# Seven products instead of eight for the third column group of the first layer, its weight sums streamed through one room

## The chip, the cores and the metric

The kernel runs on one core of a Trainium2 chip. The metric is the device time of one execution in microseconds. Before the change it is 1401.8 us, the median of three runs (1399.14 to 1404.3). The engines are named as in the profile: PE is TensorE, PEld its weight loads, DVE VectorE, ACT ScalarE, POOL GpSimd, SP the queue that issues nearly all DMAs.

## The reference

An attention with a threshold, then a bilinear feed-forward layer, all in float32:

```python
scores = scale * np.matmul(q, k.transpose(0, 1, 3, 2))          # (8, 8, 576, 576), head_dim 64
thresh = np.max(scores, axis=-1, keepdims=True) - tau
scores = np.where(scores >= thresh, scores, -1000000000.0)
attn = np.exp(scores - np.max(scores, axis=-1, keepdims=True))
attn = attn / (np.sum(attn, axis=-1, keepdims=True) + 1e-09)
attn_out = np.matmul(attn, v)
x = attn_out.transpose(0, 2, 1, 3).reshape(4608, 512)
out = ((x @ w_a) * (x @ w_b)) @ w_out                           # w_a, w_b: 512 x 1536; w_out: 1536 x 512
```

## The kernel before

**Units and slots.** Attention is cut into units of 128 query rows of a pair of heads. There are 32 pairs (batch, two heads) and 144 units; each passes through a pipeline of slots: `scores` (matmuls at L404, then row maxima L411 and thresholds L412 on DVE), `weigh` (exponential L432 on ACT, mask and sum L435 on DVE), `reciprocal` (L446, L448) and `normalise` (L454), `turn_blocks` (transposes L502 on DVE, then stores to the DRAM scratch `swap`), `turn_back` (loads into `wT`) and `weighted` (matmuls with v, "pv", L546; copies into x at L553 and L554). All matmuls are 64 x 64 pieces, four of them at a time in the four quadrants of the array; a 512-long contraction is 8 chunks of 64.

**Feed-forward blocks.** When 256 rows of x are complete (a half of a batch, or the tails of four batches), they become a block; there are 18. `exchange_blocks` makes the copy with swapped partition halves (`xs`) and, once the weight sums exist, sums of x (`x_sums`, L576) on POOL. A block is a generator, `ffn`, that yields after every few matmuls. `advance(cols)` runs it for so many columns of PE time, and the slot loop calls it in four portions per slot, so feed-forward matmuls lie between the attention's. The order on each engine is the order in which the program emits instructions (`keep_order`), so a waiting instruction holds all behind it on its engine. `held` keeps some of the columns back for the time behind pv.

**First layer.** The 1536 columns are three groups of 512 (`NG`). For a group, x times (w_a, w_b) is taken as a 2 x 2 block product: token halves and halves of the contraction on one side, halves of the contraction and the two weights on the other. Eight products would be needed; `sevens_of` does it in seven (numbered 1, 2, 6, 7, 4, 5, 3), with sums of weights (`first_sums`, L707) and sums of x. Two groups (`SEVENS`) are done so together: products 1, 6, 7, 4 are added up in one tile of on-chip accumulation memory, 2 on its own, 5 and 3 in another. ACT and DVE read the results out (L799, L803, L806, L811, L815, L820, L824), and the gated halves h are finished by DVE (product 4) and by POOL (two multiplications, L826, recorded at the helper's L712). The third group is done by `plain`: four steps, each the whole contraction for 128 columns of one weight and 256 tokens (L854, read out at L860 and L862). Three of the four steps are put between the products of the other two groups (`yield from plain(0)` to `plain(2)`), the fourth behind product 3. The sums of the two groups stay in SBUF, in `first_sb` and `more_sb`.

**The last blocks.** When attention is over (`state["over"]`), three tiles named `tw` are free; POOL computes the third group's sums into them, and `everything` does all three groups by seven products. The last two blocks go that way, 14 the way above, and the first two are plain throughout.

**Second layer.** It is also done in seven products (L920), in the pairs (1, 4), (2, 5), (7, 6) and (3), each over six pieces f, with weight sums t1, t2 and t4 in `sums_sb`. Product 1 reads the first 128 tokens of half the columns, product 4 the second 128 tokens of the other half, with t4; product 6 is the only reader of t2. Sums of h between them are on POOL (L883). The results go through tiles `kept` (tag `osb`, four rooms of 128 x 512, which the first layer's `u3` tiles use too) to DRAM.

**DMA.** `post` puts a transfer on a list and `pump` issues them on SP, each bound to the PE instruction that was last emitted; `flush` issues those at once that the next operation reads.

Of the kernel before, what the change touches and what calls it, by code (L numbers as in the profile page):

```python
# [10 lines left out]
FP32 = mybir.dt.float32  # L11
# [3 lines left out]
ALU = mybir.AluOpType  # L15
# [39 lines left out]
def kernel(  # L55
# [180 lines left out]
    for F in range(NF):  # L236
# [4 lines left out]
             "layer": False, "paced": False, "all": False, "turn": 0, "due": NPIECES, "wide": True, "slot": 0, "reading": False, "first": 0}  # L241
# [5 lines left out]
    sums_of = sums_sb.rearrange("p (f n w) -> p f n w", n=3, w=CH)  # L247
    QUARTER = HP * CH
    first_u32 = const.tile([P, 3 * QUARTER], U32, name="first_u32")
# [430 lines left out]
    def weight_sums(n, z):  # L680
        f = slice(z * NG, (z + 1) * NG)
        w = wo_sb.rearrange("p (f k) (c w) -> p f k c w", k=2, c=2)[:, f]
        w11, w12, w21, w22 = (w[:, :, k, c] for k in range(2) for c in range(2))
        t1, t2, t4 = (sums_of[:, f, m] for m in range(3))
        out, a, b = ((t1, w12, w11), (t2, w22, t1), (t4, w21, t2), (w12, w22, w12))[n]
        nc.gpsimd.tensor_tensor(out, a, b, op=ALU.subtract)


    def sums_at(group, m):
        if group == SEVENS:  # L690
            return last_sums[m]
        return (first_sb, more_sb)[group][:, m * QUARTER:(m + 1) * QUARTER]

    def last_rooms():
        for _ in range(3):
            t = work.tile([P, 2 * NB, Q], FP32, tag="tw", bufs=TW_BUFS, name="s")
            last_sums.append(t.rearrange("p n e -> p (n e)")[:, 0:QUARTER])

# [10 lines left out]
    def sevens_of(x, hg, plain):  # L709
# [13 lines left out]
        def s(m):  # L723
            return [[sums_at(NG - 1 - g, m)[:, k * CH:(k + 1) * CH] for k in range(HP)] if g >= of_all or everything
                    else None for g in range(NG)]
# [41 lines left out]
        if everything:  # L767
# [28 lines left out]
            return  # L796
        a = banks(nf * P, "pab")
# [10 lines left out]
        yield from plain(0)  # L808
# [4 lines left out]
        yield from plain(1)  # L813
# [8 lines left out]
        yield from plain(2)  # L822
# [4 lines left out]
        yield done  # L827

    def ffn(xT, what):
# [39 lines left out]
        if len(xT) == 4:  # L869
            rest = [(f, 0, HALF, (w,)) for f in range((NG - SEVENS) * n) for w in both]  # L870
            if state["all"]:
                yield from sevens_of(xT, h_of, None)
            else:
                yield from sevens_of(xT, h_of, lambda k: plain(rest[k:k + 1]))
                yield from plain(rest[3:])
        else:
            yield from plain([(*step, both) for step in steps])
# [3 lines left out]
        if state["sums"]:  # L881
# [4 lines left out]
            t1, t2, t4 = (sums_of[:, :, m] for m in range(3))  # L886
# [17 lines left out]
            for both in ((4, 1) if state["all"] else (1, 4), (2, 5), (7, 6), (3,)):  # L904
# [3 lines left out]
                for m, part in ((m, part) for m in both for part in range(1 + last)):  # L908
# [5 lines left out]
                    for f in range(NF // 2):  # L914
                        ht = hs[f // 2 * 2 + k][:, f % 2]
                        for r in range(2):
                            rows = slice(r * D, (r + 1) * D)
                            for c in range(2):
                                t0 = u * P + c * D
                                nc.tensor.matmul(po[c * D:(c + 1) * D, r, y, cut], ht[rows, t0:t0 + D],  # L920
                                                 other[rows, f, cut], start=(f == 0), stop=(f == NF // 2 - 1))
                        left -= CH // (1 + last)
                        if m == both[-1] and 4 in both and f == NF // 2 - 1:
                            h_sums((1, 1), (0, 1), (1, 1), ALU.add)
                            h_sums((0, 1), (0, 0), (0, 1), ALU.subtract)
                            h_sums((0, 0), (1, 1), (0, 0), ALU.subtract)
                        if m == 2 and f == NF // 2 - 1:
                            h_sums((1, 0), (1, 0), (0, 0), ALU.subtract)
                            state["layer"] = False
                            exchange_blocks()  # L930
                        if last and f == NF // 2 - 1:
                            for r in range(2):
                                nc.vector.tensor_tensor(final[:, cut], final[:, cut], po[:, r, 0, cut],
                                                        op=ALU.add)
                                if not part:
                                    second(r)
# [81 lines left out]
    def cost():  # L1018

        return BLOCK_COLS - (NF // 2 * CH if state["sums"] else 0) - (SEVENS * 2 * HP * P if state["first"] >= 3 * SEVENS else 0)  # L1020
# [3 lines left out]
    def advance(cols):  # L1024
        running["owed"] += cols
        while running["owed"] > 0:
            if running["ffn"] is None:
# [8 lines left out]
                if state["over"] and not state["all"]:  # L1036
                    first_sums(3, SEVENS)
                    state["all"] = True
# [73 lines left out]
    n = 0  # L1112
# [4 lines left out]
    for g in range(len(units) + PV_LAG):  # L1117
# [54 lines left out]
        if g > BY_PE:  # L1172
# [3 lines left out]
            if now:  # L1176
                held = 384 - (PORTIONS[2] + PORTIONS[3]) * pace + NSLOT * sum(width(*x) for x in now) // 2
                held = min(max(held, 0.0), 384)
# [58 lines left out]
        if g > first[HP] + 1 and not converting and state["first"] < 3 * SEVENS:  # L1237
            first_sums(state["first"] % 3, state["first"] // 3)
            state["first"] += 1
    state["over"] = True  # L1240
    last_rooms()
    for n in range(3):
        first_sums(n, SEVENS)
# [38 lines left out]
```

## Time and profile before

| what | value |
|---|---|
| median of the runs | 1401.8 us (1399.14 to 1404.3) |
| the profiled execution's own time | 1400.57 us |
| its span, first to last instruction | 1398.8 us |
| mean granted clock of TensorE | 0.998 |
| PE busy | 1361.5 us, 97% of the span |
| DVE, ACT, POOL busy | 1013.9, 680.8, 492.8 us |
| DMA moved | 223.21 MB |
| attention and feed-forward together | about 250 to 1264 us |
| feed-forward alone | about 1264 us to the end |

A busy share is the time in which an engine had an instruction under way. Line numbers (L750) are those of the kernel before. A group's line has its count, the busy time, the mean of one, and the idle time before it with what ended that. The chain is the work that ended last, followed back from the last instruction. A row of DMA issues has its count, the size of one and the median time from issue to landing.

### The profile page before, as it was taken

The numbers are of one execution on the slowest core, as the hardware profiler recorded it, in microseconds if no ns is written. First come the engines' busy times: TensorE is split into PE (matmuls) and PEld (weight loads), VectorE is DVE, ScalarE is ACT, GpSimd is POOL, SyncE is SP. The second block draws the span as 40 slices with busy tenths as digits, with TensorE's granted clock in tenths as the row PEclk, the third lists the DMA queues.
The fourth block names the chain that finished last, engine by engine and source line by source line (L and its number), as shares of the span: only waits on it lengthen the run. The fifth ranks groups of instructions, "written<-read, shape, count | busy, mean of one in ns | idle before, by whom it ended". The sixth has DMA issues, their size and how long they took to land.

```text
span 1398.8 us, 76307 instructions
## 1 busy us (share of the span) xinstructions
PE 1361.5 (97%) x33836; PEld 1258.5 (90%) x33836; DVE 1013.9 (72%) x2205; ACT 680.8 (49%) x1248; POOL 492.8 (35%) x675
## 2 busy tenths in 40 slices
PE   7889999999999999999999999999999999999998
PEld 5677588999998799999999999998899998799998
DVE  6999877787777768786767776778777776745425
ACT  6977555545554555544454545454545455431110
POOL 2764543424150607060515142332515060708100
PEclk9999999999999999999999999999999999999999
DMA  9977876667666775676556775566656775550000
GB/s 211 241 212 223 204 206 173 174 170 187 174 154 168 190 192 155 176 190 160 143 143 160 186 180 159 136 190 169 181 130 161 199 190 154 137 146 19 4 19 18
DMA packets 327449, 223.21 MB, mean 160 GB/s; under 512 B 171600, under 2 KB 311632, under 8 KB 327120
## 3 DMA queue, kind: packets, MB, share of 16 engines
q1 hardware_dynamic: 323936, 216.95, 60.1%
q8 instruction: 266, 4.36, 1.3%
q10 hardware_dynamic: 3184, 1.38, 0.4%
q14 instruction: 63, 0.52, 0.1%
HBM read 128.58 MB, written 89.65 MB: 156 GB/s over the span
## 4 chain that ended last, share of the span: by engine, by line
PE 88%; DMA 5%; DVE 4%; SPq 2%; issue 1%; ACT 1%; ACTq 0%; DVEq 0%
PE pab L750 29%; PE po L920 22%; PE pab L854 18%; PE sc L404 9%; PE pv L546 9%; SPq L144 1%; DMA vm<-in_v_dram 1%; DMA wT<-swap 1%; DVE tw L435 1%; DVE mx L411 1%; DMA more_u<-in_moe_w_a_dram 1%; DVE low L311 0%; DMA more_u<-in_moe_w_b_dram 0%; DVE tw L502 0%; DMA sums_u<-in_k_dram 0%
## 5 line engine op out<-in xcount | busy, mean ns | idle before, releaser
L454 ACT ACTIVATE tw<-tw,rcp 128x576 f32<-128x576 f32 x272 | 196.1, 768 | 201.3 <-DVE rcp L448 201.3
L411 DVE TENSOR_REDUCE mx<-sc 128x1 f32<-128x576 f32 x288 | 204.6, 752 | 121.2 <-PE sc L404 120.9
L432 ACT ACTIVATE tw<-sc,bias,scalars 128x576 f32<-128x576 f32 x288 | 239.6, 832 | 10.4 <-DMA qT<-in_q_dram 0.4
L712 POOL TENSOR_TENSOR h<-h,u 128x512 f32<-128x512 f32 x28 | 35.2, 1277 | 590.4 <-DVE h L824 414.1
L435 DVE SCALAR_TENSOR_TENSOR tw<-sc,thr,tw 128x576 f32<-128x576 f32 x288 | 220.9, 797 | 12.3 <-ACT tw L432 11.9
L920 PE MATMUL po<-wo_sb,h 64*64 64x256 f32 (+1 forms) x3408 | 210.5, 367 | 0.0
L502 DVE STREAM_TRANSPOSE tw<-tw 128x576 f32<-128x576 f32 x272 | 194.4, 752 | 0.8 <-ACT tw L454 0.8
L920 PEld LDWEIGHTS po<-wo_sb,h 64*64 64x64 f32 x3408 | 169.8, 133 | 14.9
L404 PE MATMUL sc<-kT,qT 64*64 64x288 f32 x2016 | 170.3, 404 | 1.8 <-issue 0.9
L546 PE MATMUL pv<-wT,vm 64*64 64x128 f32 (+2 forms) x4896 | 164.0, 275 | 3.7 <-DMA vm<-in_v_dram 1.4
L546 PEld LDWEIGHTS pv<-wT,vm 64*64 64x64 f32 x4896 | 153.2, 133 | 12.0 <-issue 4.0
L920 PE MATMUL po<-sums_u,h 64*64 64x256 f32 x2448 | 156.6, 376 | 0.0
L883 POOL TENSOR_TENSOR h<-h 128x256 f32<-128x256 f32 x168 | 117.2, 731 | 110.9 <-PE po L920 106.1
L750 PE MATMUL pab<-xU,wb_sb 64*64 64x128 f32 x4352 | 137.8, 269 | 0.0
L920 PEld LDWEIGHTS po<-sums_u,h 64*64 64x64 f32 x2448 | 126.1, 133 | 12.3 <-DVE h L862 0.5
L750 PEld LDWEIGHTS pab<-xU,wb_sb 64*64 64x64 f32 x4352 | 133.3, 133 | 1.8 <-ACT h L806 0.5
L404 PEld LDWEIGHTS sc<-kT,qT 64*64 64x64 f32 x2016 | 108.8, 133 | 17.3 <-issue 4.9
L431 ACT ACTIVATE bias<-mx,scalars 128x1 f32<-128x1 f32 x288 | 82.7, 287 | 66.1 <-DVE mx L411 65.6
L553 ACT COPY xT<-pv 128x128 f32<-128x128 f32 (+1 forms) x68 | 17.6, 259 | 193.5 <-PE pv L546 193.5
L750 PE MATMUL pab<-xS,wa_sb 64*64 64x128 f32 x2176 | 108.5, 269 | 0.8 <-issue 0.8
L554 DVE COPY xT<-pv 64x128 f32<-64x128 f32 (+1 forms) x136 | 38.1, 280 | 80.5 <-PE pv L546 79.0
L535 ACT COPY kept<-po 128x512 f32<-128x512 f32 x65 | 34.8, 535 | 120.3 <-PE po L920 106.4
(163 smaller groups left out, 2468.7 us busy)
## 6 DMA issues: line engine op xcount, KB each, us to landing
wT<-swap SPq DMA_DIRECT2D x242, 288.0 KB, 3.8
swap<-tw SPq DMA_DIRECT2D x480, 144.0 KB, 3.1
vm<-in_v_dram SPq DMA_DIRECT2D x128, 72.0 KB, 2.6
swap<-tw SPq DMA_DIRECT2D x128, 72.0 KB, 2.9
kT<-in_k_dram SPq DMA_DIRECT2D x112, 72.0 KB, 3.2
wT<-swap SPq DMA_DIRECT2D x56, 144.0 KB, 3.6
out_dram<-kept SPq DMA_DIRECT2D x27, 256.0 KB, 3.7
qT<-in_q_dram SPq DMA_DIRECT2D x112, 40.0 KB, 2.8
```

The costliest lines, as they stand in the source:

```text
L404: nc.tensor.matmul(sc[m][o * D:o * D + wide, c], qT[r, q0:q0 + wide], kT[r, c * SH:(c + 1) * SH], start=True, stop=True)
L411: nc.vector.tensor_reduce(mx[:, c], sc[j], axis=AX.XY, op=ALU.max)
L431: nc.scalar.activation(bias[:, j:j + 1], mx[:, j:j + 1], AF.Copy, scale=e_nscale)
L432: nc.scalar.activation(wb[j], sb[j], AF.Exp, bias=bias[:, j:j + 1], scale=e_scale)
L435: nc.vector.scalar_tensor_tensor(out=wv, in0=sb[j], scalar=thr[:, j:j + 1], in1=wv, op0=ALU.is_ge, op1=ALU.mult, accum_out=sums[:, j:j + 1])
L454: nc.scalar.activation(w, w, AF.Copy, scale=rcp[:, j:j + 1])
L502: nc.vector.transpose(w, w)
L546: nc.tensor.matmul(pv[c * D:(c + 1) * D, y], vm[rows, s], wT[y](rows, s), start=(s == 0), stop=(s == NSLOT - 1))
L750: nc.tensor.matmul(out[c * D:(c + 1) * D, r, f * P:(f + 1) * P], w[g][k][rows, w0:w0 + D], moving[k][rows], start=(fresh and k == 0 and f ...
L854: nc.tensor.matmul(pab[c:c + columns(), r], w[rows, f // n, k, fs + c:fs + c + columns()], moving, start=(k == 0), stop=(k == H - 1))
L883: (nc.vector if state["over"] else nc.gpsimd).tensor_tensor(*a, **kw)
L920: nc.tensor.matmul(po[c * D:(c + 1) * D, r, y, cut], ht[rows, t0:t0 + D], other[rows, f, cut], start=(f == 0), stop=(f == NF // 2 - 1))
```

## The change

The third group is done by seven products in the 14 blocks as well. For each product the two accumulated results of a kind are not added up in accumulation memory across products; each product is read out by itself and the sums are made in SBUF (`alone`). The pieces are put where the plain steps were: products 6 and 1, then 7 and 5, then 2 and 4, and product 3 by itself behind product 3 of the other two groups.

Its three weight sums are computed once by POOL, early, in `more_sb`, and stored in the DRAM scratch `streamed`, with a copy of two thirds of t2. That part of t2's place (`stream_sb`, 512 KB) is the one room into which `stream(m)` reads them: sum 1 for product 6, then sum 0 for product 5, then sum 2 for product 3, then t2 again for the second layer, and sum 1 for the next block behind the second layer's product 6. Each reload is two DMAs on SP. The sums in `sums_sb` lie one behind the other for this (t1, t4, t2). In these blocks the second layer goes through its pieces f in descending order. The last blocks read their sums from `streamed` into the `tw` tiles. `cost()` counts one group more, and `held` can go up to 640 columns in place of 384.

```diff
+    t1, t4, t2 = (sums_sb[:, c:c + NF // 2 * CH].rearrange("p (f w) -> p f w", w=CH)
+                  for c in range(0, NSUM, NF // 2 * CH))
+    stream_sb = sums_sb[:, NSUM - QUARTER:]
+    streamed = scratch.tile([4, P, QUARTER], FP32, tag="streamed", bufs=1, name="streamed")
...
     def sums_at(group, m):
         if group == SEVENS:
-            return last_sums[m]
+            return (last_sums[m] if state["all"] else stream_sb if state["third"] > 2 else
+                    more_sb[:, m * QUARTER:(m + 1) * QUARTER])
...
+    def stream(m):
+        if state["held"] != m:
+            for c in range(0, QUARTER, QUARTER // 2):
+                nc.sync.dma_start(stream_sb[:, c:c + QUARTER // 2], streamed[m, :, c:c + QUARTER // 2])
+        state["held"] = m
...
+        single = state["third"] > 4
+        s_t, u_t = ((work.tile([P, 2 * nf // SEVENS * P], FP32, tag="osb", bufs=OSB_BUFS, name="u3")
+                     .rearrange("p (r f n) -> p r f n", r=2, n=P) for _ in range(2)) if single else (None, None))
+
+        def alone(*ms):
+            size = 2 * len(one) * P
+            ps = banks(len(ms) * size, "pab")
+            halves = [ps[:, :, n * size:(n + 1) * size] for n in range(len(ms))]
+            for n, m in enumerate(ms):
+                yield from product(m, halves[n], n == 0, True, one)
+                if m in (6, 5, 3):
+                    stream({6: 0, 5: 2, 3: 3}[m])
+                if n < len(ms) - 1:
+                    yield P, size * HP, len(ms) * size * HP
+            z = {m: split(x) for m, x in zip(ms, halves)}
+            if 6 in z:
+                nc.scalar.copy(g1, z[6])
+                nc.scalar.copy(g0, z[1])
+                pool(g1, g1, g0, op=ALU.add)
+            if 7 in z:
+                nc.scalar.copy(u_t, z[7])
+                pool(u_t, u_t, g1, op=ALU.add)
+            if 5 in z:
+                nc.scalar.copy(s_t, z[5])
+            if 5 in z:
+                pool(g1, g1, s_t, op=ALU.add)
+                pool(s_t, s_t, u_t, op=ALU.add)
+            if 2 in z:
+                nc.vector.tensor_tensor(g0, g0, z[2], op=ALU.add)
+            if 4 in z:
+                nc.vector.tensor_tensor(u_t, u_t, z[4], op=ALU.add)
+            if 4 in z:
+                (nc.vector if state["over"] else nc.gpsimd).tensor_tensor(g0, g0, u_t, op=ALU.mult)
+            if 3 in z:
+                nc.vector.tensor_tensor(g1, g1, z[3], op=ALU.add)
+                pool(g1, g1, s_t, op=ALU.mult)
+            yield done
+
+        def between(k):
+            return alone(*((6, 1), (7, 5), (2, 4))[k]) if single else plain(k)
...
-        yield from plain(0)
+        yield from between(0)
...
+        if single:
+            yield from alone(*(3,))
...
-                yield from plain(rest[3:])
+                if state["third"] < 5:
+                    yield from plain(rest[3:])
...
-                    for f in range(NF // 2):
+                    order = range(NF // 2)[::-1] if state["third"] > 4 and not state["all"] else range(NF // 2)
+                    for f in order:
...
+                        if m == 6 and f == order[-1] and state["third"] > 4 and not state["over"]:
+                            stream(1)
...
-                if state["over"] and not state["all"]:
+                if len(blocks[0][0]) == 4 and state["third"] == 4:
                     first_sums(3, SEVENS)
-                    state["all"] = True
+                    state["third"] += 1
+                state["all"] = state["over"]
+                if state["third"] > 4:
+                    stream(3 if state["all"] else 1)
...
-                held = 384 - (PORTIONS[2] + PORTIONS[3]) * pace + NSLOT * sum(width(*x) for x in now) // 2
-                held = min(max(held, 0.0), 384)
+                most = 640 if state["third"] > 4 else 384
+                held = most - (PORTIONS[2] + PORTIONS[3]) * pace + NSLOT * sum(width(*x) for x in now) // 2
+                held = min(max(held, 0.0), most)
...
         if g > first[HP] + 1 and not converting and state["first"] < 3 * SEVENS:
+            if state["third"] < 3:
+                n = state["third"]
+                first_sums(n, SEVENS)
+                nc.sync.dma_start(streamed[n], sums_at(SEVENS, n))
+                state["third"] += 1
+            elif state["third"] == 3:
+                nc.sync.dma_start(streamed[3], stream_sb)
+                state["third"] += 1
             first_sums(state["first"] % 3, state["first"] // 3)
             state["first"] += 1
     state["over"] = True
     last_rooms()
     for n in range(3):
-        first_sums(n, SEVENS)
+        nc.sync.dma_start(last_sums[n], streamed[n])
```

## The prediction

> **What bounds the kernel now.** I read the busy times first, then stretches, then the chain.
>
> ```profile
> PE   1361.5 (97%) x33836; PEld 1258.5 (90%) x33836; DVE 1013.9 (72%) x2205; ACT 680.8 (49%) x1248; POOL 492.8 (35%) x675
> ...
> 300.00:400.00 100.00, 100.00 (x2463) 94.01 (x2458) 78.33 (x173) 51.32 (x94) 42.12 (x66) 1.00 0.68 178
> 600.00:700.00 100.00, 99.57 (x2449) 97.13 (x2444) 72.00 (x158) 45.47 (x82) 43.84 (x67) 1.00 0.62 163
> 900.00:1000.00 100.00, 99.46 (x2514) 89.59 (x2510) 76.65 (x167) 51.63 (x95) 45.60 (x71) 1.00 0.68 175
> ```
>
> The columns of a stretch are its length, then PE, PEld, DVE, ACT and POOL busy, granted clock, DMA share, GB/s. From 250 to 1264 us, where all 14 blocks of the edited path run, PE has almost no idle time: each microsecond of matmul taken away counts, and each one that PE waits is lost. DVE has about a quarter left, POOL over half, DMA a third. The chain of waits gives the rates:
>
> ```profile
> 190.24 7.34 PE pab L854 x136
> ...
> 540.47 6.91 PE po L920 x128
> ...
> 700.83 8.66 PE pab L750 x312
> ...
> 1282.07 28.87 PE pab L750 x1052
> ```
>
> Start, length, what. A matmul instruction leaves two records. 256 columns cost 54.0 ns a record (7.34/136, 6.91/128), 128 columns 27.4 to 27.8 (28.87/1052, 8.66/312).
>
> **What is removed.** A plain pass of the third column group is 4 steps of 8 chunks of 4 quadrants: 128 instructions, 256 records (L854 has 3584 in this stretch, 14 x 256): 256 x 54.0 = 13.82 us. Seven products are 7 x 2 x 4 x 4 = 224 instructions, 448 records: 12.27 to 12.43 us. Each block saves 1.39 to 1.55 us, 14 blocks 19.5 to 21.6; I take **20.5**. The two last blocks have this already. The third group's sums need four slots and the other two groups' need six in the same stretch of slots, so the flag is set before the first such block and all 14 do switch.
>
> **The room's reloads.** Each block reads four sums of 512 KB, as two issues of 256 KB: about 112 issues, 29 MB; with the saved sums about 33 MB on 223. At the main queue's own mean (60.1% for 216.95 MB) that is 9 points of DMA share at most: 0.65 becomes 0.74, no bound.
>
> ```profile
> wT<-swap SPq DMA_DIRECT2D x242, 288.0 KB, 3.8
> ...
> out_dram<-kept SPq DMA_DIRECT2D x27, 256.0 KB, 3.7
> raw<-in_moe_w_a_dram SPq DMA_DIRECT2D x14, 256.0 KB, 8.4
> ...
> raw<-in_moe_w_out_dram SPq DMA_DIRECT2D x6, 512.0 KB, 4.4
> ...
> sums_u<-in_moe_w_out_dram SPq DMA_DIRECT2D x3, 512.0 KB, 5.3
> ```
>
> Last figure: us to landing. A reload starts when the product that reads the room ends, so what matters is the PE work until the next reader. Shortest is the one behind product 6: product 1 (1.75), seven of the pair (3.5), seven of the third group (1.75): 7.0 us, plus what attention puts between. In the trace, the same distance (middle of the first plain step to middle of the second) is 7.9 us or more in 13 blocks, 6.9 in one. The others have 13 us and more. The reload takes two issues on SP (0.36 to 0.45 each) and a landing: nearest by size and kind are the 512 KB weight rows, 4.4 to 5.3 us, taken at a DMA share over 0.8; the far end is the 256 KB row of 8.4. SP is at most 2.3 us into other issues there. 1 + 0.8 + 5 = 6.8 against 7.9: mostly hidden. **1 us** in all; ends 0 and 14 x 2 = 28 (8.4 + 0.45 + 1 = 9.9, 2.0 over 7.9). On SP, the paced copies behind a reload (swap, wT, q, k, v) wait for later PE work anyway; 112 x 0.4 = 45 us of issue lie in its idle time.
>
> **The end of the first layer.** This is where I expect the loss. Product 4 of the second layer needs the paired groups' gated tokens: product 3, DVE's add, POOL's two multiplications.
>
> ```profile
> 528.68 0.51 DVE L365 STREAM_TRANSPOSE qT<-qT 128x320 f32<-128x320 f32 x1
> 529.11 1.18 DVE L824 TENSOR_TENSOR h<-h,pab 128x1024 f32<-128x1024 f32 x1
> ...
> 530.37 2.52 POOL L712 TENSOR_TENSOR h<-h,u 128x512 f32<-128x512 f32 x2 [47.21 <-DVE sums L446]
> ```
>
> Here product 3 ended at 525.8, DVE came to its add 3.3 us late, POOL ended 7.1 us after it. Before, 3.45 us of plain step, 2.6 of product 1 and two column pieces (0.86) lie between: 6.9. After, the single product 3 lies there (1.75), product 1 (2.6), and the reversed order asks for the last POOL half first: 4.35. Without lag the chain takes 3.86 (1.21 + 2 x 1.28 + handovers). I took the same three times (last record of product 3, end of L824, end of the second L712) for all 14 blocks: nine have scores or pv in the 4.4 us behind product 3 and so more cover; the five without overrun it by 0, 0.7, 2.8, 0.9 and 0.4. **4.8 us**; ends 0 (attention falls in between) and 14 x 1.5 = 21. The third group's own last multiplication (1.28) is needed 1.73 us later and fits.
>
> **DVE, ACT, POOL.** A block loses two ACT copies and two DVE multiplications and gets four copies (0.58), three DVE adds (0.68) and six POOL operations as L712 (1.28). ACT +16 us, DVE +10, POOL +107 in 1014 us (10.6%). DVE's small operations wait for POOL:
>
> ```profile
> 299.15 2.50 POOL L712 TENSOR_TENSOR h<-h,u 128x512 f32<-128x512 f32 x2 [37.84 <-DVE h L824]
> ...
> 300.44 1.24 DVE L412 TENSOR_SCALAR thr<-mx,scalars 128x2 f32<-128x2 f32 x1
> ...
> L412 DVE TENSOR_SCALAR thr<-mx,scalars x144: 228/229/1803, 11.7 to 1232.0; 128x2 f32<-128x2 f32 x144
> ...
> L446 DVE TENSOR_SCALAR sums<-sums x136: 124/169/1173, 14.1 to 1235.0; 128x2 f32<-128x2 f32 x136
> ```
>
> L412 usually takes 0.23; this one ended when POOL did, at 301.7. Of 113 x 2 such operations 10.6% would hit an added POOL operation, with 0.64 left: 15 us more on DVE. It has idle time (L411 waits 102 us for scores in this stretch), so I put **2 us** on PE; ends 0 and 15. The Trainium skill (SBUF — State Buffer, SBUF: two separate sides) says the same in general: a port pair shared by VectorE and GpSimd is locked for a whole instruction and "the loser **fully blocks**". Taken for every two-port VectorE operation this would stretch the large ones too; here the trace disagrees, L502 takes 748 ns beside POOL and 753 alone. By the rule DVE would lose up to POOL's whole 107 us.
>
> **Buffers, start, end.** The third group takes two more of the four 128x512 rooms, so it waits for the stores of the block before. In the trace these land before the end of the second plain step, where such a room would first be written, in 13 blocks (by 0.4 to 15 us), and 1.9 after it in one, where ACT would wait: **1 us**, ends 0 and 4 (2 blocks). Three POOL sums (2.4 each) and four 512 KB stores move to 180 to 220 us, where SP issues without pause and L412 once waited 1.8: **1.5**, ends 0 and 5. At the end the same three sums leave POOL and come by DMA; PE did not wait for them, so nothing is gained. The raised hold of 640 columns only moves 256 columns from before pv to after it: 0, ends -2 and +2, since PE stays covered on both sides.
>
> **Sum.** -20.5 + 1 + 4.8 + 2 + 1 + 1.5 = -10.2. The profiled execution took 1400.6 (span 1398.8 and 1.8 around it), 1.2 under the median of 1401.8; so 1390.4, or **1391** as a median.
>
> **The rivals.**
> A, forecast: as above, 1385 to 1394.7.
> B, nothing reaches PE: attention fills each gap. 1401.8 - 20.5 = 1381. For it: nine of 14 blocks already have cover. Against: the five overruns.
> C, DVE falls behind: the 15 us of blocked DVE all reach PE, 13 more than taken: 1404. For it: DVE at 72 to 78%, in bursts (3.3 us late above). Against: 102 us of idle before L411 alone.
> D, the other side: the first reload lands late in every block. At 8.4 us landing it costs 28 instead of 1: 1418. It decides from 17 us, 1.2 a block, a landing 9.1 us after product 6 ends. For it: the 8.4 row, same size, and DMA at 0.74. Against: that row is from the start, at a share above 0.8, while 512 KB landed in 4.4 there and wT in 3.8 here.
> A further rule speaks against the change: the Trainium skill (TensorE: Matmul & The Clock Gate, LDWEIGHTS) gives columns/1.2 ns for a weight load, 53 ns for 64 columns as an estimate; 192 more loads in each of 14 blocks would end any gain. The trace has a load with each 27.4 ns record, so it does not hold here, and I give it no chance.
>
> **Chances.** 0.5% of 1401.8 is 7 us, about what can be told from no change. A 0.48, B 0.17 (both faster: 0.65), C 0.20 (1395 to 1408: same), D 0.15 (slower). The range 1379 to 1408 holds A, B and C; A alone is 1385 to 1394.7.
>
> **What would show it.** L854 without records from 250 us on, and 6272 more in L750. In the chain, PE waits at L920 for POOL's multiplication of some microseconds in all (A); none (B). PE waits at L750 for a DMA into the sums tile only if D is right, and then about 2 us in each block. L412 and L446 longer in the mean, and PE waiting for DVE's L435: C. DMA bytes near 256 MB. The prediction fails if PE idles over 17 us in the stretch, or if the matmuls that read the streamed room take more than 27.8 ns a record.

## The result, and the profile after

The changed kernel takes 1457.0 us (median of four runs, 1453.4 to 1457.9), the kernel before, run beside it, 1402.4 (1399.1 to 1404.3). The ratio is 1.038, 95% interval 1.0356 to 1.0404. It is slower by 55 us; 1391 was forecast. The two profiled spans are 1456.1 and 1398.8, so 57.3 us are to be found.

The page of the changed kernel, first its busy times, then its DMA rows and its chain of work that ended last:

```profile
PE 1370.1 (94%) x36476; PEld 1232.3 (85%) x36476; DVE 1035.0 (71%) x2215; ACT 695.1 (48%) x1277; POOL 599.0 (41%) x760
...
DMA packets 344464, 256.60 MB, mean 176 GB/s; under 512 B 173488, under 2 KB 313264, under 8 KB 344112
...
q8 instruction: 287, 4.70, 1.4%
...
PE 81%; DVE 7%; DMA 4%; issue 4%; SPq 2%; POOL 1%; ACT 0%; ACTq 0%; DVEq 0%; POOLq 0%
...
sums_u<-streamed SPq DMA_DIRECT2D x112, 256.0 KB, 4.0
```

The same rows of the page before:

```profile
q8 instruction: 266, 4.36, 1.3%
...
PE 88%; DMA 5%; DVE 4%; SPq 2%; issue 1%; ACT 1%; ACTq 0%; DVEq 0%
```

PE fell from 97% to 94% of a longer span. The chain had 1% of "issue" before (time in which the engine waited for nothing that the profile shows) and has 4% now; DMA's share of it did not rise. The reloads land in 4.0 us. The stretches of 100 us answer the ones shown of before, with one more (length, then PE, PEld, DVE, ACT and POOL busy, granted clock, DMA share, GB/s):

```profile
300.00:400.00 100.00, 96.10 (x2682) 87.88 (x2678) 76.97 (x163) 47.65 (x87) 38.82 (x50) 0.98 0.72 194
500.00:600.00 100.00, 94.39 (x2746) 86.87 (x2741) 71.93 (x156) 51.09 (x90) 38.02 (x51) 1.00 0.71 201
600.00:700.00 100.00, 94.08 (x2717) 84.08 (x2707) 70.86 (x154) 46.81 (x86) 36.30 (x47) 1.00 0.71 191
900.00:1000.00 100.00, 95.89 (x2831) 86.10 (x2828) 70.35 (x154) 48.64 (x90) 37.34 (x47) 1.00 0.66 178
```

In the stretches shown of before PE was 99.5 to 100 us busy; in these it is idle 4 to 6 of 100, and 2.3 to 2.9 in the two best ones between 300 and 1300 us. POOL has over half its time left and DVE more than before, so no other engine has become the bound. The waits of PE name what ended them (line, releaser, us in total, times, longest); L760 is the products' matmul, L550 pv, L408 the scores, L974 the second layer:

```profile
PEld pab L760 <- issue: 50.6, 77, 2.2
...
PE pab L760 <- issue: 32.5, 49, 2.0
...
PEld pab L760 <- DMA sums_u<-streamed: 5.8, 4, 3.7
...
PEld po L974 <- POOL h L723: 1.8, 3, 0.9
```

Before, the first of these rows was:

```profile
PEld pab L750 <- issue: 6.4, 12, 1.2
```

The waits that the prediction spoke of are there and small: 5.8 us for the reloads in four waits, 1.8 us for POOL. The large one has no releaser. (PE and PEld rows overlap, so they are not added.) To count each idle time once, I took the gaps over 250 ns between the end of one weight load and the start of the next; what is left between starts of weight loads I call spacing.

| stage, us | before | after |
|---|---|---|
| start to the first seven-product matmul | 251.1 | 256.9 |
| from there to the last pv: spacing | 996.3 | 990.7 |
| the same stretch: gaps without a releaser | 8.8 | 63.6 |
| the same stretch: other gaps | 3.9 | 10.5 |
| behind the last pv | 138.8 | 134.5 |

The gaps without a releaser account for 54.8 of the 57.3 us. Their place is seen in the chain, in order of time (start, length, what, records):

```profile
678.15 0.60 issue
...
679.89 3.20 PE pab L760 x108
683.09 0.50 issue
683.59 3.72 PE pab L760 x128
687.31 1.13 issue
688.43 2.08 PE pab L760 x67
```

Between two stalls lie exactly 128 records. A record is a weight load and a matmul, so that is 256 instructions. The page's row q8 gives 287 instruction transfers, 4.70 MB: 16,384 bytes each, which for 256 instructions is 64 bytes apiece. In the trace 79 gaps without a releaser (59.9 us) end 1.1 to 1.8 us after such a transfer of q8; 74 of them lie at one and the same position, PE instruction number 193 to 197 modulo 256. Before, there were 11 such gaps, 7.0 us. I call them page-end stalls. The Trainium skill (Runtime: NRT & Kernel Launch, Instruction fetch mechanics) says that an engine's instructions come in blocks of 16 KiB, 256 instructions, by a DMA queue of its own, and that crossing a block is mostly hidden. The size and the position agree with this trace; that it is hidden held before the change and does not hold after it.

Behind the last pv, with a DMA share of 0.04, the same boundaries show with almost no stall:

```profile
1364.85 0.02 issue
1364.87 3.72 PE pab L760 x128
1368.59 0.02 issue
1368.61 7.39 PE pab L760 x257
```

A page lasts 3.7 us there. In the attention stretch, where two stalls follow each other by one page, the time from the one resume to the next is 4.51 us in the median (32 pairs). And what PE asks for can be counted from the records, two instructions each: from the first seven-product matmul to the last pv at least 25,985 records in 996.3 us of spacing before, one page per 4.91 us; 28,779 in 990.7 us after, one page per 4.41 us. On the mean, the change moved the demand past the 4.51 us of these pairs; a stalled page itself was worked off in 3.51 us (the pairs' median without the stall), so it is in runs of narrow records that PE outpaces the supply.

### The profile page after: what moved, and what is told of

It reads as the page before. It is cut to its first block, busy times and chain, and to the rows that moved or that the text cites. A ratio compares the mean times of both kernels' runs of the same rounds, so it can differ in the third digit from the quotient of the medians.

```text
span 1456.1 us, 81974 instructions
## 1 busy us (share of the span) xinstructions
PE 1370.1 (94%) x36476; PEld 1232.3 (85%) x36476; DVE 1035.0 (71%) x2215; ACT 695.1 (48%) x1277; POOL 599.0 (41%) x760
## 2 busy tenths in 40 slices
DMA packets 344464, 256.60 MB, mean 176 GB/s; under 512 B 173488, under 2 KB 313264, under 8 KB 344112
## 4 chain that ended last, share of the span: by engine, by line
PE 81%; DVE 7%; DMA 4%; issue 4%; SPq 2%; POOL 1%; ACT 0%; ACTq 0%; DVEq 0%; POOLq 0%
PE pab L760 40%; PE po L974 20%; PE pv L550 9%; PE sc L408 9%; PE pab L907 3%; DVE tw L439 1%; SPq L144 1%; DVE mx L415 1%; DMA wT<-swap 1%; DVE low L315 1%; DVE tw L506 1%; DMA qT<-in_q_dram 1%; DMA sums_u<-streamed 1%; DMA raw<-in_moe_w_b_dram 1%; DMA vm<-in_v_dram 1%
## 5 line engine op out<-in xcount | busy, mean ns | idle before, releaser
L415 DVE TENSOR_REDUCE mx<-sc 128x1 f32<-128x576 f32 x288 | 204.5, 752 | 143.0 <-PE sc L408 142.9
L760 PE MATMUL pab<-xU,wb_sb 64*64 64x128 f32 x6144 | 204.4, 271 | 14.3 <-issue 14.1
L974 PE MATMUL po<-wo_sb,h 64*64 64x256 f32 (+1 forms) x3360 | 207.8, 370 | 0.4 <-issue 0.3
L760 PEld LDWEIGHTS pab<-xU,wb_sb 64*64 64x64 f32 x6144 | 187.8, 133 | 22.9 <-issue 21.2
L974 PEld LDWEIGHTS po<-wo_sb,h 64*64 64x64 f32 x3360 | 153.9, 133 | 29.2 <-issue 2.1
L408 PE MATMUL sc<-kT,qT 64*64 64x288 f32 x2016 | 171.7, 408 | 6.0 <-issue 4.4
L550 PE MATMUL pv<-wT,vm 64*64 64x128 f32 (+2 forms) x4896 | 165.0, 277 | 7.9 <-issue 4.5
L550 PEld LDWEIGHTS pv<-wT,vm 64*64 64x64 f32 x4896 | 151.4, 134 | 18.0 <-issue 12.7
L974 PE MATMUL po<-sums_u,h 64*64 64x256 f32 x2448 | 152.2, 377 | 0.6 <-POOL h L723 0.5
L760 PE MATMUL pab<-xS,wa_sb 64*64 64x128 f32 x3072 | 147.2, 270 | 4.9 <-issue 4.7
L937 POOL TENSOR_TENSOR h<-h 128x256 f32<-128x256 f32 x168 | 116.3, 735 | 70.4 <-PE po L974 70.1
L974 PEld LDWEIGHTS po<-sums_u,h 64*64 64x64 f32 x2448 | 111.8, 133 | 24.4 <-POOL h L723 1.8
L760 PE MATMUL pab<-xT,wa_sb 64*64 64x128 f32 x2688 | 129.3, 271 | 1.1 <-issue 0.8
L408 PEld LDWEIGHTS sc<-kT,qT 64*64 64x64 f32 x2016 | 103.8, 134 | 27.8 <-issue 12.5
L760 PEld LDWEIGHTS pab<-xS,wa_sb 64*64 64x64 f32 x3072 | 118.7, 133 | 6.9 <-issue 5.9
L760 PEld LDWEIGHTS pab<-xT,wa_sb 64*64 64x64 f32 x2688 | 104.3, 133 | 4.7 <-issue 2.0
```

The source lines that it names most:

```text
L408: nc.tensor.matmul(sc[m][o * D:o * D + wide, c], qT[r, q0:q0 + wide], kT[r, c * SH:(c + 1) * SH], start=True, stop=True)
L415: nc.vector.tensor_reduce(mx[:, c], sc[j], axis=AX.XY, op=ALU.max)
L550: nc.tensor.matmul(pv[c * D:(c + 1) * D, y], vm[rows, s], wT[y](rows, s), start=(s == 0), stop=(s == NSLOT - 1))
L760: nc.tensor.matmul(out[c * D:(c + 1) * D, r, f * P:(f + 1) * P], w[g][k][rows, w0:w0 + D], moving[k][rows], start=(fresh and k == 0 and f ...
L937: (nc.vector if state["over"] else nc.gpsimd).tensor_tensor(*a, **kw)
```

## The experiments

The theories. F: PE runs out of instructions, because records of 128 columns use up a page twice as fast as those of 256, and the pages come no faster. L: the traffic of the reloads is the cause. W: small records cost more in themselves. P (for the last three runs): it is PE's own side that cannot take a page faster, whatever DMA does. Ratios are to runs of the kernel before on the same chip, taken beside each run.

| kernel | median us | ratio, 95% interval | PE records | page-end stalls: number, us |
|---|---|---|---|---|
| before | 1402.4 | | 33,836 | 11, 7.0 |
| after | 1457.0 | 1.038 [1.0356, 1.0404] | 36,476 | 79, 59.9 |
| e1_no_reload | 1443.0 | 1.0227 [1.0183, 1.0272] | 36,476 | 82, 59.2 |
| e2_cut | 1462.0 | 1.0355 [1.0312, 1.0397] | 37,420 | 67, 43.5 |
| e3_wide_third | 1444.0 | 1.0212 [1.0149, 1.0275] | 33,340 | 35, 20.9 |
| e4_wide_all | 1434.4 | 1.0158 [1.0110, 1.0207] | 25,724 | 12, 5.3 |
| f1_cut_wide | 1435.4 | 1.0228 [1.0197, 1.0260] | 33,836 | 9, 4.5 |
| f2_cut_half | 1416.6 | 1.0096 [1.0061, 1.0130] | 35,628 | 18, 8.7 |
| f3_reload_only | 1424.8 | 1.0147 [1.0116, 1.0179] | 33,836 | 20, 18.9 |
| f4_wide_mixed | 1436.2 | 1.0230 [1.0198, 1.0262] | 26,216 | 0, 0.0 |
| g1_quiet_after | 1420.9 | 1.0120 [1.0091, 1.0149] | 36,476 | 46, 32.3 |
| g2_quiet_before | 1397.8 | 0.9958 [0.9942, 0.9973] | 33,836 | 5, 3.3 |
| g3_quiet_no_reload | 1413.4 | 1.0060 [1.0039, 1.0081] | 36,476 | 48, 28.1 |

Stalls are counted from 240 us on, by their time behind a transfer, and so take in some others by chance: at the page position itself lie 74 of the changed kernel's 79 (57.5 us), 29 of e3's 35 (18.2 us) and none of e4's 12.

### e1_no_reload: the change without its reloads

```diff
     def stream(m):
-        if state["held"] != m:
+        if False:
```

> The changed kernel without its reloads: nothing is ever read into the streamed room, so products 6, 5 and 3 of the third group take whatever lies there (t2's columns) and the output is not the reference's; the four stores early and all matmuls, ACT, DVE and POOL work stay. Theory F (PE runs out of instructions: its program comes in pages of 256 instructions, and a long run of 128-column matmuls eats a page in 3.5 us, as fast as a page can be fetched): PE's idle time that ends by no shown releaser stays near 60 us (at least 45), only the 5.6 us of waits for the reloads go; 1443 to 1455 us. Theory L (the 29 MB of reloads are what delays PE, by their own landing or by crowding the fetches): that idle time falls to about 10 us; 1385 to 1400 us.

Still 2.3% slower than before; faster than the changed kernel by 14 us by the medians and by 21 by the two ratios (1.038 and 1.0227 of 1402), since the two were not run beside each other. The page-end stalls are the same (59.2 against 59.9 us), with the DMA share down from 0.71 to 0.64 to 0.66:

```profile
PEld pab L760 <- issue: 50.9, 79, 1.9
```

So the stalls do not need the reloads: L falls as the main cause. Of the 13.6 us between the two spans 5.6 are the waits for the reloads; the rest is spread over stages, none over 3.4.

### e2_cut: the kernel before with its plain 256-column matmuls cut in two

```diff
+                            cuts = (0, P) if len(xT) == 4 else (0,)
+                            size = (c1 - c0) // len(cuts)
                             for c in range(0, P, columns()):
-                                nc.tensor.matmul(pab[c:c + columns(), r],
-                                                 w[rows, f // n, k, fs + c:fs + c + columns()], moving,
-                                                 start=(k == 0), stop=(k == H - 1))
+                                for e in cuts:
+                                    nc.tensor.matmul(pab[c:c + columns(), r, e:e + size],
+                                                     w[rows, f // n, k, fs + c:fs + c + columns()],
+                                                     moving[:, e:e + size],
+                                                     start=(k == 0 and e == 0),
+                                                     stop=(k == H - 1 and e == cuts[-1]),
+                                                     skip_group_check=len(cuts) > 1)
```

> The kernel before, with one edit: in the 14 blocks (and only there) each 256-column matmul of the third group's plain steps is issued as two of 128 columns with the same weights. Same sums, no reload, no added ACT, DVE or POOL work. Theory F: the first layer becomes one long run of 128-column matmuls as in the changed kernel, with 512 records a block in place of 448; idle time without a shown releaser grows from 20 to 60 us or more; 1440 to 1470 us. Theory L, and a theory P by which POOL's added work holds up DVE: 1400 to 1412 us, since a 128-column record costs 27.4 to 27.8 ns and a 256-column record 54.0.

None of the change is in it: no reload, no copy, no sum more. It multiplies the same columns in 3584 records more, and is as slow as the change. That the totals agree so closely is partly chance, since the parts differ: page-end stalls rose from 7.0 to 43.5 us, 64 of 67 at the same position, and the spacing of the cut matmuls from 182.9 to 210.2 us; this second part is a price of the records themselves. All idle time without a releaser rose from 18.8 to 56.3 us over the whole execution, a little short of F's 60. Both rows name no releaser:

```profile
PEld pab L750 <- issue: 21.8, 39, 1.9
...
PEld pab L857 <- issue: 18.5, 34, 1.3
```

The stalls hit the untouched products at L750 as well as the cut steps at L857: they go by the count of instructions, not by the line.

### f1_cut_wide: cut, but with as many instructions as before

The same cut, with 64 x 128 pieces, so that the number of records is again that of before.

```diff
+                            step = P if len(cuts) > 1 else columns()
-                            for c in range(0, P, columns()):
...
+                            for c in range(0, P, step):
...
```

> The kernel before with the plain steps of the 14 blocks cut into 128-column matmuls as in e2_cut, but in pieces of 64 rows by 128 weight columns: as many instructions as before, as many matmuls of 128 columns as in e2_cut. Theory F (the number of instructions, not the width of a matmul, makes PE wait): stalls at a page's end 15 us or less against 43.5 in e2_cut and 7.0 before; 1405 to 1435 us, the excess over before being the price of changing between 64-wide and 128-wide pieces (18 us of smaller gaps and 18 of gaps near 0.44 us in e3_wide_third). Theory W (a run of 128-column matmuls is slow by itself, by its weight loads): as e2_cut, 40 us or more of stalls at a page's end, 1455 us or more.

The page-end stalls go from 43.5 to 4.5 us, and PE has no idle time in the stretches in which e2_cut had 2.4 to 3.0 us (e2_cut first, then f1_cut_wide):

```profile
500.00:600.00 100.00, 96.99 (x2868) 93.65 (x2863) 70.36 (x156) 50.02 (x89) 24.71 (x37) 1.00 0.63 165
600.00:700.00 100.00, 97.61 (x2861) 94.64 (x2857) 69.95 (x155) 44.90 (x81) 26.80 (x39) 1.00 0.66 167
```

```profile
500.00:600.00 100.00, 100.00 (x2562) 88.75 (x2560) 72.23 (x159) 50.45 (x92) 24.68 (x37) 1.00 0.62 169
600.00:700.00 100.00, 100.00 (x2410) 85.43 (x2411) 68.91 (x153) 44.37 (x80) 32.96 (x48) 1.00 0.63 163
```

Records of 128 columns do not stall PE; too many instructions do. The time stays at 1435, the upper end of what F gave, for another reason: a 64 x 128 piece costs more in this stretch, 62.3 ns a record (219.2 us for 3520), against 52.0 for a 256-column record of the same work.

### f2_cut_half: half of the cut

As e2_cut, but only the steps of w_a are cut (`len(xT) == 4 and w is wa_sb`).

> e2_cut with only two of the four plain steps of a block cut (those of w_a, between products 6 and 7 and between 5 and 3), in 64 by 64 pieces. Theory F: the long run of narrow matmuls is broken by two plain steps, at which the fetching catches up; stalls at a page's end between before (7.0) and e2_cut (43.5) and under the middle of the two, 12 to 25 us; 1412 to 1435 us. Theory W: exactly half of the loss of e2_cut, 25 to 30 us over before.

Half of the cuts cost 1.0%, all of them 3.6%. The stalls are 8.7 us against 43.5 and the 7.0 of the kernel before, so somewhat fewer than the 12 to 25 that F gave. A price per record would be half; a supply that is overrun gives less than half at first. For the stalls that speaks for F and against W. W does hold for the spacing of the plain steps: it rose by 12.8 us (182.9 to 195.7), near half of e2's 27.3, and this is most of what f2 loses.

### e3_wide_third and e4_wide_all: fewer instructions for the change

The products in 64 x 128 pieces, half as many instructions for the same columns: in e3 those of the third group, in e4 all.

```diff
-                        for c in range(2):
-                            w0 = y * P + c * D
-                            nc.tensor.matmul(out[c * D:(c + 1) * D, r, f * P:(f + 1) * P],
-                                             w[g][k][rows, w0:w0 + D], moving[k][rows],
+                        step = P if state["third"] > 4 and not everything and len(groups) == 1 else D
+                        for c in range(0, P, step):
+                            w0 = y * P + c
+                            nc.tensor.matmul(out[c:c + step, r, f * P:(f + 1) * P],
+                                             w[g][k][rows, w0:w0 + step], moving[k][rows],
...
```

(e4: `step = P`.)

> The changed kernel, with the third group's single products in pieces of 64 rows by 128 weight columns, one instruction in place of two, 224 records a block in place of 448. Such pieces cost 55 to 57 ns a record in the early stage of the kernel before, twice a 64 by 64 record, so the time of the matmuls themselves should hardly change. Theory F: a page lasts twice as long in those products, idle time without a shown releaser falls from 80 us (whole execution) to 20 to 40; 1395 to 1420 us. Theories L and P: nothing changes, 1450 to 1462 us.

> The changed kernel, with all seven-product matmuls of the first layer, of all three groups and of the last two blocks too, in pieces of 64 by 128. Theory F: no page is eaten faster than in about 7 us any more, idle time without a shown releaser falls under 15 us; with the 11 to 20 us of saved matmul time 1375 to 1395 us, less some us if the wide pieces cost 57 in place of 55 ns. Theories L and P: 1450 to 1462 us.

The stalls at the page ends went as F says, 59.9 to 20.9 to 5.3, none of the last 12 at the page position. The times missed the upper ends by 24 and 39 us, and so did all idle time without a releaser: 49.7 and 49.2 us over the whole execution, where 20 to 40 and under 15 were expected. The waits of e4 show why:

```profile
PEld pab L761 <- issue: 42.0, 114, 0.4
```

Many short waits, the longest 0.4 us. 82 of all gaps without a releaser last 0.38 to 0.445 us, 35.7 us together: 76 where a wide piece follows scores, 6 where it follows the second layer, none behind pv. The 12 that the table counts are among them. A wide record takes 58.6 ns in the stretch (551.1 us for 9408), two narrow ones 57.5 (540.9 for 18,816), so nothing is gained back by width.

### f4_wide_mixed: the switch itself

e4 with the first chunk behind other PE work in 64 x 64 pieces, so that no wide piece follows directly.

```diff
+                    step = P if newest() == mine[0] else D
...
-                        for c in range(2):
...
+                        for c in range(0, P, step):
...
+                    mine[0] = newest()
```

> e4_wide_all, with the first chunk of a product behind other work on PE (scores, pv, second layer) in 64 by 64 pieces, so that its weight loads need not wait for both column halves of the array. If the 70 gaps near 0.44 us of e4_wide_all are that wait, they go, and 10 to 25 us with them: 1410 to 1425 us. If the wait only moves to the change from narrow to wide pieces behind that chunk: 1430 to 1440 us.

The 0.44 us waits are gone, and so are all page-end stalls, but the products' spacing rose by 37 us (588.4 against 551.1). The cost of wide pieces between narrow ones was moved, not removed, as the second alternative had it. What it consists of I did not separate. None of these variants beats the kernel before.

### f3_reload_only: the memory traffic alone

The change's sums, stores and reloads at the places of the plain steps, with the third group done by `plain` as before. The order of f, `cost()` and the held columns are those of before too.

```diff
+        single, reload = False, state["third"] > 4
         def between(k):
-            return alone(*((6, 1), (7, 5), (2, 4))[k]) if single else plain(k)
+            yield from plain(k)
+            if reload and k < 2:
+                stream((0, 2)[k])
...
+                yield from plain(rest[3:])
+                if state["third"] > 4:
+                    stream(3)
```

> The change's memory traffic without its products: the third group goes by plain steps as before, while the room is filled with its sums at the changed kernel's places (behind plain steps 0, 1 and 3 and behind the second layer's product 6) and the early sums, stores and the last blocks' loads are the changed kernel's; nothing reads the room but t2's readers. Theory F and the prediction's term for the reloads: 0 to 6 us over before, 1402 to 1410; stalls at a page's end 7 to 12 us. Theory L: a large part of the change's loss, 1430 us or more.

A miss: 21 us slower than before, where 1402 to 1410 was expected. The spacing is that of before (997.5 against 996.3), and no wait for a reload appears among PE's. The page-end stalls rose from 7.0 to 18.9 us, all 20 at the page position, and the stage ahead of the first product took 5.5 us longer (256.6 against 251.1; kernels with the same work there range from 251.0 to 254.4). The early sums and stores are part of this run, so not all of the 21 us is the reloads'. PE has no record more than before, and in the attention stretch most of the loss there is longer page-end stalls: the added traffic slows the supply of instructions. e1 had not shown this; why the stalls stayed there without the reloads, perhaps because the demand was so high, is not shown.

### g1_quiet_after, g2_quiet_before: most stores to swap left out

```diff
+    stored = {}
     def turn_blocks(i, u):
-        swap = scratch.tile([G, P, NSLOT * Q], FP32, tag="swap" if u < NT else "swapt", name="swap")
-        swaps[i, u] = swap
+        new = (i % HP, u) not in stored
+        if new:
+            stored[i % HP, u] = scratch.tile([G, P, NSLOT * Q], FP32, tag=f"swap{i % HP}_{u}", bufs=1, name="swap")
+        swap = swaps[i, u] = stored[i % HP, u]
...
-            post(("tw", i, u), *moves)
+            post(("tw", i, u), *(moves if new else ()))
```

> The changed kernel without most of the stores to the scratch `swap`: only the first unit of each (pair modulo 4, query part) is stored, and all later units of that kind read what it left, so the output is not the reference's. The loads into wT, the reloads of sums and all work on the engines stay. It asks what makes the fetching of PE's instructions slow in the attention stretch. Theory F (the fetches, 16 KB each, share the DMA engines with the data): with some 65 MB of stores gone the pages come as fast as in the phase without attention; the stalls at the ends of pages fall from 59.9 us to under 25, and the time to 1395 to 1425. Theory P (it is PE's own sequencer that cannot take a page in less than 4.3 to 4.7 us when products, scores and pv alternate): the stalls stay at 50 to 65 us and the time at 1440 to 1457.

> The kernel before with the same stores left out, for comparison (output likewise not the reference's). F: it has only 7.0 us of stalls at the ends of pages to lose, so 1385 to 1402, and the changed kernel without stores stands within 20 us of it, in place of 55. P: the distance between the two stays at 45 to 60 us.

The DMA share of the changed kernel fell from 0.71 to 0.45 to 0.47, and PE's idle time from some 6 to 2 or 3 of 100 us:

```profile
500.00:600.00 100.00, 98.17 (x2915) 95.96 (x2911) 74.17 (x165) 53.20 (x97) 37.45 (x47) 1.00 0.45 129
600.00:700.00 100.00, 97.40 (x2775) 87.64 (x2769) 76.72 (x161) 46.55 (x84) 41.45 (x54) 1.00 0.47 124
```

The time fell by 36 us (1457.0 to 1420.9) with all of PE's work kept, that of the kernel before by 5.7 (1403.5 to 1397.8): the distance between the two went from 55 to 23 us, the stalls from 59.9 to 32.3. Of the 37 us between the two spans 28 are gaps without a releaser, and 6.4 are waits that end with one. The distance and the stalls are close to F's numbers (20 and 25) without reaching them, and P's (45 to 60, and 50 to 65) are far. The load on DMA carries about half of the stalls.

### g3_quiet_no_reload: both left out

g1 with the `if False` of e1.

> The changed kernel without most of the stores to `swap` and without the reloads of the streamed room as well (output not the reference's). All of PE's work stays. The run with the stores alone left out had a DMA share of about 0.48 in the attention stretch, 32.3 us of stalls at the ends of pages and 1420.9 us. If those stalls go with the DMA load (F), another 29 MB less brings the share to about 0.40, the stalls to 15 to 27 us and the time to 1396 to 1412. If what is left is PE's own limit (P), or depends on something other than the amount moved, the stalls stay at 29 to 36 us, and the time falls only by what the reloads cost otherwise: 1408 to 1418.

The second alternative, nearly: 28.1 us of stalls and 1413.4 us, at a DMA share of 0.39 to 0.46. Less traffic still hardly shortens them. What the other half comes from stays open. The time from resume to resume over single stalled pages is 4.51 us in the changed kernel, 4.05 in g1 (13 pairs) and 4.27 in g3 (12 pairs), against 3.7 where DMA is nearly idle and products run alone. The transfer itself took a median of 0.96, 1.06 and 0.94 us in these pairs; what grew is the time from one transfer's end to the next one's start (3.45, 3.06 and 3.20 us), for which the trace has no record. Counted from PE's resuming, the next transfer starts 2.00, 1.53 and 1.72 us later. In g1 and g3 a stalled page thus came faster than the mean demand of the change (4.41 us), and 46 and 48 stalls stayed: it is not the mean that decides, but the runs of records in which PE works a page off in 3.5 us.

## Why the prediction was wrong

**What bounds the kernel** was read rightly, and the forecast's own condition met: it was to fail if PE idled over 17 us in the stretch, and PE idled 74.1 there (63.6 of it without a releaser). The step that failed is one that the sum did not have: an added instruction was priced by the time of its record alone. The sum took 192 records more per block at the time that they need on PE, and a rule on their weight loads was weighed; that PE must also fetch them was put at nothing, without a reason. What the runs showed in its place: page-end stalls rose from 7.0 to 59.9 us, they appear when the old matmuls are merely cut (e2, 43.5 us), and they go when the cut keeps the number of instructions (f1, 4.5 us). The number was on the page: 33,836 records, 266 pages; 192 records in each of 14 blocks are 21 pages more, and 287 were fetched. None of the rivals A to D had this mechanism. D had the direction, but its own cause, reloads that land late, measured 5.6 us in place of 28.

**Matmul saving, -20.5.** Mis-sized. The products and plain steps together went from 624.1 us of spacing (L750 364.0 and 74.0, L854 182.9 and 3.2) to 615.3 (L760 540.9 and 74.4): -8.8, where the forecast had -20.5. The rates of 54.0 and 27.4 to 27.8 ns had been read from short undisturbed pieces of the chain, two of them outside the stretch. Over the whole stretch the trace of before gives a spacing of 52.0 ns for 256 columns (182.9 us for 3521) and 29.0 for 128 (364.0 for 12,544): 14 x (256 x 52.0 - 448 x 29.0) ns = 4.5 us. With these the saving was too small for the price of the rest, and the forecast would have been no change. The Trainium skill's rule (TensorE: Matmul & The Clock Gate, LDWEIGHTS), by which weight loads would eat the gain and to which I gave no chance, is not what happened: with a load in every record, 128 columns took 27.7 ns behind the last pv (74.4 us for 2688).

**Reloads, +1 (ends 0 and 28).** The mechanism was half right: they land in 4.0 us, and PE waits only 5.6 us for them (D's place). But leaving them out gave 14 to 21 us (e1), and f3, which has the early sums and stores as well, is 21 us slower than before. In f3's attention stretch most of the price is longer page-end stalls (7.0 to 18.9 us).

**End of the first layer, +4.8.** The waits at L974 for POOL's multiplication are 1.8 us, near the lower end. That attention and the next product cover more than the sample of three times suggested is the likely reason; I did not follow it block by block.

**DVE, +2.** DVE's two small operations beside POOL grew as forecast:

```profile
L416 DVE TENSOR_SCALAR thr<-mx,scalars 128x2 f32<-128x2 f32 x144 | 58.4, 405 | 5.1
L450 DVE TENSOR_SCALAR sums<-sums 128x2 f32<-128x2 f32 x136 | 37.5, 276 | 2.2
```

Before, these were:

```profile
L412 DVE TENSOR_SCALAR thr<-mx,scalars 128x2 f32<-128x2 f32 x144 | 47.7, 331 | 5.1
...
L446 DVE TENSOR_SCALAR sums<-sums 128x2 f32<-128x2 f32 x136 | 30.3, 223 | 2.2
```

Together they take 17.9 us more; 15 were forecast. It does not reach PE: the gaps in the stretch that DVE ended are 2.2 us, and DVE's own idle time before the row maxima rose from 120.9 to 142.9 us, since it waits for PE. C falls. The prediction tested how DVE and POOL hinder each other on L502 alone, a transpose with one input. An operation with two inputs from SBUF does stretch: in the changed kernel DVE's 128x256 operations at L937 took 422 ns in the mean without a POOL operation beside them (42 of them) and 823 with one beside them for over half their time (11).

**Buffers, +1, and start, +1.5.** 1.3 us of the gaps come from the read-out into `kept`, so the first holds. The start took 5.8 us longer, a little over the upper end of 5, with some 3 us of scatter between kernels with equal work there.

**Held columns, 0.** The part behind pv is 4.3 us shorter, with 88 second-layer records fewer (1063 against 1151); work only moved.

**What was to be seen.** The plain steps' records (L907 now) end at 234 us and the products have 6272 more (21,504 against 15,232), the bytes are 256.6 MB for some 256. These were right and say nothing on the time.

## What to carry to other kernels

Before a matmul is split, or replaced by more and smaller ones, count instructions per microsecond next to columns per microsecond: a bound engine that just kept up with its instruction pages (here one per 4.9 us) may not keep up with 10% more (one per 4.4 us), and fewer multiplications then run slower. Stalls with no releaser that lie a fixed number of records apart are the sign, and the quick test is to cut the old matmuls in two with everything else untouched. Take the rate of an instruction from the whole stretch in which it will run, not from its fastest piece.

## What the runs showed of the hardware

PE's instructions arrive in transfers of 16,384 bytes, 256 instructions. Alone, with DMA nearly idle, PE used a page of 128 records in 3.7 us with 0.02 us between pages; with attention running at a DMA share near 0.7 consecutive stalled pages were 4.5 us apart, although the transfer itself took 1 us in both. At the page position, PE resumed 1.2 to 1.8 us after a transfer's end.

DMA traffic lengthened PE's time by more than the waits for it: 33 MB more in f3 went with 11.9 us more of page-end stalls and no wait of PE for a reload, and 70 MB of stores taken away (256.60 MB in all to 186.88) took 27.6 us of such stalls from the changed kernel, of 36 us in all, and gave the kernel before 5.7.

A 64 x 128 piece that follows 64 x 64 pieces waited by what it follows: in e4 0.44 us behind scores in all 77 cases, 0.17 to 0.23 us behind pv in all 32. A wide record cost 58.6 ns in e4's attention stretch and 62.3 in f1's, against 56.1 behind it in e4 (75.4 us for 1344).
